# Attention scores divided at half the queries, products in other bursts, and loads in another order, in a fused attention and maxout feed-forward kernel

## The chip, the cores and the metric

One core of a Trainium2 chip runs the whole program. The metric is the device time of one execution in microseconds; the kernel before takes 307.9 us (median of three runs, 307.81 to 308.14). The engines are named as in the profile: PE multiplies matrices (PEld is its loading of weights), ACT evaluates functions such as Exp and Ln, DVE and POOL work on tiles elementwise, and SP issues transfers. ACT and POOL also issue transfers; those of POOL can convert float32 to bfloat16 on the way.

## The reference, cut to what matters

```python
# q, k, v: [8, 8, 576, 64]; beacon_k, beacon_v: [8, 8, 16, 64]
k_all = concatenate([beacon_k, k], axis=2)           # 592 keys
scores = scale * q @ k_all^T                         # beacons are seen by all, the rest causally
a = exp(scores - max); a /= a.sum(-1) + 1e-9
x = (a @ v_all) -> [8*576, 8*64]                     # 4608 tokens of 512
h = maximum(maximum(x @ w1, x @ w2), x @ w3)         # [4608, 768]
out = h @ w_out                                      # [4608, 512]
```

## The kernel before

**Quads.** The heads of a batch are taken four at a time. There are 16 such quads Q (two to a batch); PE works on four heads at once, each on 32 of its rows (scores) or 32 of its columns (products). Keys lie on the partitions in five tiles t of 128 (the last has 80 rows), queries along the free axis. `turn` lets DVE transpose the loaded q and k of a quad into `qT` and `kT`, in four pieces per quad.

**Four bursts to a quad.** `emit_scores(Q, c)` computes one burst c of the scores on PE (first 496 columns for each head, then 368, 464 and 336), ACT takes the exponential into `at_sb` in two instructions of two heads each, and POOL sets what a query may not see to zero (`affine_select`). `bursts` says which key tile and which range of queries belong to each burst.

**Products.** `pv_pass(Q, hf, part)` takes one half `hf` of the queries (288). Part 0 multiplies by ones and gives the row sums: ACT takes Ln and then Exp of its negative, which leaves the reciprocal in `recip`. Parts 1 and 2 multiply by v (even and odd columns) and DVE multiplies the result by `recip` into `xT` (L292). The first half of the queries costs 512 columns of PE in a pass, the second 1152. `PV_ORDER` makes three steps of two passes each, done in bursts 1, 2 and 3 of the next quad: both sums, then the two products of the first half, then the two of the second. Results lie in the tile `pv`, of which `pv_psum` holds two; a third pass reuses the buffer of the pass two before it.

**Feed-forward units.** When a batch is through attention, its tokens go through the feed-forward part in units of four to six products: `mm1_unit` (L311; i = 0 is copied by ACT, L319; i = 1 and 2 are joined by DVE, L321) and `mm2_unit` (L328; DVE copies the result to `y`, L336, and SP sends it out). There are 198 units of them. Unit results have two buffers, `fps`. `emit_all` writes the order of the work out by hand: in each burst it lets as many units follow as a counter allows (two per burst in quads 2 to 4, then 2.8), interleaved with the entries of `plan` (transposes, casts and loads, set by `at_step(Q, c, ...)`). Every engine runs its instructions in the order in which they are written.

**Opening.** `begin` loads q and k of quads 0 and 1 by SP in float32 and casts them on ACT, DVE and POOL; later quads come through POOL's queue with conversion (`load_qk16`, two to three quads ahead). V comes by SP in float32 (`load_v`) and is cast by POOL. Feed-forward units begin with quad 2.

Of the kernel before, what the change touches and what calls it, by code (L numbers as in the profile page):

```python
# [16 lines left out]
def kernel(  # L17
# [13 lines left out]
    nc = tc.nc  # L31
# [85 lines left out]
    def load_beacon_k(b0, b1, queues):  # L117
        for g, queue in enumerate(queues):
# [5 lines left out]
    def cast_beacon_k(b0, b1, cast):  # L124
        cast(bk16[:, b0:b1], bk32[:, b0:b1])

    def turn_beacon_k(b0, b1):
        nc.vector.transpose(
            bkT[:, b0:b1].rearrange("p b n e -> p (b n e)").bitcast(U32),
            bk16[:, b0:b1].rearrange("p b d -> p (b d)").bitcast(U32),  # L130
        )
# [66 lines left out]

    def load_w(i):
        wv = (moe_w1, moe_w2, moe_w3)[i].rearrange("(g p e) f -> p g (e f)", g=n_quad, e=2)  # L200
        nc.gpsimd.dma_start(out=w_in[i].rearrange("p (g e) f -> p g (e f)", e=2), in_=wv)
# [8 lines left out]
    def emit_scores(Q, c):  # L210
# [5 lines left out]
        off = 0  # L216
        for t, q0, q1 in bursts[c]:
            w = q1 - q0
            for j in range(2):
                for h in range(HG):  # L220
                    hs = slice(32 * h, 32 * h + 32)
                    nc.tensor.matmul(  # L222
                        sc[h // 2][:, h % 2, off : off + w],
                        kT[hs, 128 * t : 128 * (t + 1), j],
                        qT[hs, q0:q1, j],
                        start=(j == 0),
                        stop=(j == 1),
                        tile_position=(32 * h, 0),
                    )
            off += w  # L230
        a0, a1 = burst_at[c]
        for i in range(HG // 2):
            nc.scalar.activation(  # L233
                out=at_sb[:, 2 * i : 2 * i + 2, a0:a1],
                in_=sc[i][:, :, 0:off],
                func=AF.Exp,
                scale=scale,
            )
        off = a0
        for t, q0, q1 in bursts[c]:  # L240
            edge = min(q1, 128 * t - Nb + k_rows[t])
            if q0 == q_min[t]:
# [15 lines left out]
    def pv_pass(Q, hf, part):  # L258
# [25 lines left out]
        if part == 0:  # L284
# [4 lines left out]
            recips[hf] = recip  # L289
        else:  # L290
            c0 = b % RING * S + h0
            nc.vector.tensor_mul(xT[:, 2 * g + part - 1, c0 : c0 + HALF], ps, recips[hf])  # L292

    PV_ORDER = [(0, 0), (1, 0), (0, 1), (0, 2), (1, 1), (1, 2)]

    def emit_pv(Q, step):
        for hf, part in PV_ORDER[2 * step : 2 * step + 2]:
            pv_pass(Q, hf, part)
# [75 lines left out]
    def begin():  # L374
        load_beacon_k(0, 1, (nc.scalar, nc.gpsimd))
        load_qk(0, 1, (0, SH, QS))
        load_qk(0, 0, (0, SH, QS))
        load_qk(1, 1, (0, QS))
        load_qk(1, 0, (0, QS))
        load_v(0)  # L380
        cast_beacon_k(0, 1, by_pool)
        for which in (1, 0):
            for s0, s1 in ((0, SH), (SH, QS)):
                cast_qk(0, which, by_act, s0, s1)
                turn(0, which, s0, s1)
            if which == 1:
                turn_beacon_k(0, 1)
                put_beacon_k(0, by_dve)
                put_beacon_k(1, by_dve)
        cast_qk(1, 1, by_dve)  # L390
        turn(1, 1, 0, SH)
        turn(1, 1, SH, QS)
        cast_qk(1, 0, by_pool)
        load_beacon_k(1, B, (nc.sync, nc.sync))

    at_step(0, 0, L(turn, 1, 0, 0, SH), L(turn, 1, 0, SH, QS))
    at_step(0, 2, L(load_qk16, 2, 1), L(load_qk16, 2, 0), L(cast_v, 0, 0, 2, by_dve))
    at_step(0, 3, L(load_w, 0), L(cast_v, 0, 2, 4, by_dve))
    at_step(1, 0, L(cast_v, 0, 4, 5, by_pool), L(load_w, 1))
    at_step(1, 1, L(load_w, 2), L(cast_beacon_k, 1, B, by_pool), L(turn_beacon_k, 1, B))  # L400
    at_step(1, 2, L(load_qk16, 3, 1), L(load_qk16, 3, 0), L(load_v, 1))
    at_step(1, 3, L(load_w_out))
    for Q in range(2, NQ):
        b, g = divmod(Q, n_quad)
        at_step(Q - 1, 1 if Q > 2 else 3, L(turn, Q, 1, 0, SH))
        at_step(Q - 1, 2, L(put_beacon_k, Q, by_pool))
        at_step(Q - 1, 2 if Q > 2 else 3, L(turn, Q, 1, SH, QS), L(turn, Q, 0, 0, SH))
        at_step(Q - 1, 3, L(turn, Q, 0, SH, QS))
        if Q >= 4:
            at_step(Q - 3, 3, L(load_qk16, Q, 1), L(load_qk16, Q, 0))  # L410
        if g == 1:
            if b >= 2:
                at_step(Q - 4, 3, L(load_v, b))
# [4 lines left out]
    def emit_all():  # L418
# [8 lines left out]
        for Q in range(NQ):  # L427
            b, g = divmod(Q, n_quad)
            for c in range(NC):
                if Q == n_quad and c == 0:  # L430
                    for step in range(3):
                        emit_pv(Q - 1, step)
                    ready = 0
                elif Q > 0 and c > 0 and Q != n_quad:
                    emit_pv(Q - 1, c - 1)
                emit_scores(Q, c)
# [3 lines left out]
                allowed += early_rate if step in early else rate if step >= early.stop else 0.0  # L440
                for fn in plan.pop((Q, c), ()):
# [6 lines left out]
        assert not plan, list(plan)  # L448
        for step in range(3):
            emit_ffn(len(units), B - 2)  # L450
            emit_pv(NQ - 1, step)
# [38 lines left out]
```

## Time and profile before

| | before |
|---|---|
| median of three runs | 307.9 us |
| the profiled execution: time, span | 308.23 us, 306.5 us |
| PE busy | 278.5 us, 91% of the span |
| DVE, ACT, POOL busy | 54%, 52%, 29% |
| first feed-forward product | 36.82 us |
| chain that ended last: PE, ACT, transfers | 76%, 11%, 5% |
| PE's idle time before scores, unit products, attention products (v, ones) | 14.2, 6.6 and 1.7, 1.6 us |

The span is what the trace covers; 1.7 us of the execution's own time lie around it. In a row of a timeline stand the start, the time, the engine, the line, the operation, what it writes and reads, and in brackets the idle time of the engine just before, with what ended it. A row can merge several instructions; their count follows the x.

### The profile page before, as it was taken

The page shows a single profiled execution, that of the slowest core. Times are in us where ns is not written, and L with a number is a line of the kernel's source. Part 1 is how long each engine was busy: PE and PEld are TensorE (multiplying, and loading weights), DVE is VectorE, ACT ScalarE, POOL GpSimd, SP SyncE. Part 2 cuts the span into 40 slices and gives each one's busy share as a digit, 9 for nine tenths or more (in the row PEclk, how much of TensorE's full clock was granted, in tenths as well). Part 3 has the DMA queues.
Part 4 walks back from the last instruction along what each step waited for, and adds up shares of the span by engine and source line. Part 5 has one row for each costly group of instructions (what it writes and reads, how often), then busy time and mean ns, then how long its engine had stood idle before and what let it go on. Part 6 is the DMA issues. An engine that isn't in the chain of part 4 may idle for free.

```text
span 306.5 us, 7641 instructions
## 1 busy us (share of the span) xinstructions
PE 278.5 (91%) x3240; PEld 136.9 (45%) x3240; DVE 164.9 (54%) x282; ACT 159.2 (52%) x251; POOL 88.2 (29%) x159
## 2 busy tenths in 40 slices
PE   0477799998999999998999889999999999999995
PEld 0233534443454444443445657444444445444442
DVE  2603436855665566664647364755456456455553
ACT  4475597655765485645564637357545741220210
POOL 3356345434232432242323413242204210000000
PEclk9999999999999999999999999999999999999999
DMA  7979999995941495239333664250021002102103
GB/s 253 214 127 216 209 200 200 184 264 113 177 72 52 117 179 95 58 112 183 53 75 139 114 123 79 105 107 8 3 86 53 2 2 79 60 0 103 36 0 138
DMA packets 51650, 33.65 MB, mean 110 GB/s; under 512 B 41120, under 2 KB 41888, under 8 KB 51616
## 3 DMA queue, kind: packets, MB, share of 16 engines
q1 hardware_dynamic: 45728, 21.73, 28.7%
q0 software_dynamic: 5760, 11.42, 21.6%
q8 instruction: 25, 0.41, 0.6%
q14 instruction: 9, 0.07, 0.1%
q10 hardware_dynamic: 128, 0.02, 0.0%
HBM read 35.13 MB, written 9.44 MB: 145 GB/s over the span
## 4 chain that ended last, share of the span: by engine, by line
PE 76%; ACT 11%; DMA 5%; SPq 4%; DVE 1%; issue 1%; POOL 1%; DVEq 0%
PE fps L311 35%; PE fps L328 13%; PE pv L276 13%; PE sc L222 9%; ACT at_sb L233 7%; PE sc L311 5%; SPq L184 2%; DMA vst<-in_v_dram 2%; ACT hT L319 2%; PE sc L328 2%; DMA st<-in_q_dram 2%; DMA out_dram<-y 1%; SPq L122 1%; ACT lnd L286 1%; DVE xT L292 1%
## 5 line engine op out<-in xcount | busy, mean ns | idle before, releaser
L311 PE MATMUL fps<-xT,w_sb 128*128 128x512 bf16 (+1 forms) x648 | 140.1, 356 | 6.6 <-ACT hT L319 4.6
L233 ACT ACTIVATE at_sb<-sc 128x992 bf16<-128x992 f32 (+3 forms) x128 | 103.6, 863 | 76.9 <-PE sc L222 76.9
L321 DVE TENSOR_TENSOR hT<-hT,fps 128x512 bf16<-128x512 bf16 x96 | 65.9, 687 | 78.3 <-PE fps L311 46.7
L311 PEld LDWEIGHTS <-w_sb 128*128 128x128 bf16 x720 | 66.3, 98 | 81.0 <-issue 23.6
L245 POOL TENSOR_SCALAR_AFFINE_SELECT at_sb<-at_sb 128x512 bf16<-128x512 bf16 (+2 forms) x80 | 46.5, 590 | 150.5 <-ACT at_sb L233 150.4
L222 PE MATMUL sc<-qT,kT 32*128 32x288 bf16 (+4 forms) x768 | 41.1, 300 | 14.2 <-DVE qT L166 9.4
L319 ACT CAST hT<-fps 128x512 bf16<-128x512 f32 x48 | 28.1, 598 | 34.5 <-PE fps L311 34.4
L328 PE MATMUL fps<-w_out_sb,hT 128*128 128x512 bf16 x192 | 44.6, 380 | 0.0
L336 DVE COPY y<-fps 128x512 f32<-128x512 f32 x32 | 22.1, 692 | 21.5 <-PE fps L328 19.9
L276 PE MATMUL pv<-at_sb,v_sb 128*32 128x288 bf16 (+4 forms) x1024 | 31.4, 267 | 1.7 <-DVE xT L292 1.6
L328 PEld LDWEIGHTS <-hT 128*128 128x128 bf16 x216 | 20.3, 98 | 26.0 <-issue 2.7
L276 PEld LDWEIGHTS <-v_sb 128*32 128x32 bf16 (+1 forms) x1024 | 23.1, 101 | 16.7 <-issue 13.8
L222 PEld LDWEIGHTS <-kT 32*128 32x128 bf16 x768 | 16.2, 96 | 31.8 <-issue 17.0
L292 DVE TENSOR_TENSOR xT<-pv,recip 128x288 bf16<-128x288 f32 x64 | 26.9, 449 | 6.4 <-PE pv L276 3.9
L166 DVE STREAM_TRANSPOSE kT<-c 128x256 uint32<-128x256 uint32 (+1 forms) x32 | 22.2, 709 | 7.0 <-ACT c L159 3.5
L166 DVE STREAM_TRANSPOSE qT<-c 128x256 uint32<-128x256 uint32 (+1 forms) x32 | 21.8, 701 | 1.7 <-POOL c L159 1.4
L192 POOL CAST v_sb<-vst 128x1024 bf16<-128x1024 f32 (+1 forms) x22 | 19.4, 881 | 3.1 <-DMA vst<-in_v_dram 3.1
L311 PE MATMUL sc<-xT,w_sb 128*128 128x512 bf16 x72 | 18.5, 380 | 0.0
L286 ACT ACTIVATE lnd<-pv 128x288 f32<-128x288 f32 x32 | 12.9, 405 | 8.8 <-PE pv L276 8.7
L276 PE MATMUL pv<-at_sb,ones 128*32 128x288 bf16 (+4 forms) x512 | 16.0, 268 | 1.6 <-POOL at_sb L245 1.6
L276 PEld LDWEIGHTS <-ones 128*32 128x32 bf16 (+1 forms) x512 | 11.0, 100 | 9.7 <-issue 8.2
L288 ACT ACTIVATE recip<-lnd 128x288 f32<-128x288 f32 x32 | 14.2, 443 | 1.0
(24 smaller groups left out, 53.1 us busy)
## 6 DMA issues: line engine op xcount, KB each, us to landing
out_dram<-y SPq DMA_DIRECT2D x36, 256.0 KB, 2.0
vst<-in_v_dram SPq DMA_DIRECT2D x24, 256.0 KB, 5.4
c<-in_k_dram POOLq DMA_DIRECT2D x14, 288.0 KB, 4.4
c<-in_q_dram POOLq DMA_DIRECT2D x14, 288.0 KB, 5.3
w_sb<-in_moe_w_dram POOLq DMA_DIRECT2D x3, 768.0 KB, 10.6
vst<-in_v_dram SPq DMA_DIRECT2D x8, 224.0 KB, 4.5
vst<-in_v_dram SPq DMA_DIRECT2D x8, 160.0 KB, 6.1
w_out_sb<-in_moe_w_out_dram POOLq DMA_DIRECT2D x1, 768.0 KB, 14.6
```

What stands on the lines that cost most here:

```text
L166: nc.vector.transpose(dst.rearrange("p (t s) -> p s t", s=RUN)[:, s0:s1], src.rearrange("p (s d) -> p s d", d=DP),)
L192: cast(v_tiles[b][0:n, t0:t1].rearrange("p t h d -> p (t h d)"), stage["v", b][0:n, t0:t1].rearrange("p t h d -> p (t h d)"),)
L222: nc.tensor.matmul(sc[h // 2][:, h % 2, off : off + w], kT[hs, 128 * t : 128 * (t + 1), j], qT[hs, q0:q1, j], start=(j == 0), stop=(j == 1 ...
L233: nc.scalar.activation(out=at_sb[:, 2 * i : 2 * i + 2, a0:a1], in_=sc[i][:, :, 0:off], func=AF.Exp, scale=scale,)
L245: nc.gpsimd.affine_select(out=view, in_=view, compare_op=ALU.is_ge, fill=0.0, base=q0 - (128 * t - Nb), pattern=[[0, HG], [1, edge - q0]], ...
L276: nc.tensor.matmul(ps[32 * j : 32 * j + 32, lo - h0 : hi - h0], lhsT, at_sb[0:n, j, a : a + hi - lo], start=(i == 0), stop=(i == len(runs) ...
L292: nc.vector.tensor_mul(xT[:, 2 * g + part - 1, c0 : c0 + HALF], ps, recips[hf])
L311: nc.tensor.matmul(ps[:, o0 : o0 + n], w_in[i][:, ct, 128 * ft : 128 * (ft + 1)], xT[:, ct, x0 : x0 + n], start=(ct == 0), stop=(ct == n_c ...
L319: nc.scalar.copy(hT[:, ft, :], ps)
L321: nc.vector.tensor_max(hT[:, ft, :], hT[:, ft, :], ps)
L328: nc.tensor.matmul(ps, hT[:, ft, 128 * tt : 128 * (tt + 1)], w_out_sb[:, ft, :], start=(ft == 0), stop=(ft == n_ft - 1),)
L336: nc.vector.tensor_copy(y, ps)
```

## The change

**Bursts divided at half the queries.** A quad's four bursts are now: the first half of the queries for key tiles 0, 1 and 2 (512 columns per head), then the second half for tiles 0 and 3 (496), for tiles 1 and 4 (368) and for tile 2 (288). The total is the same, in eight pieces and not six, and six masks and not five. In quads 0 and 1 PE does two heads of a burst after the other two; from quad 2 on all four together as before.

**Products in other bursts.** From quad 3 on, burst 1 holds both products of the first half of the quad before, and then its sums of the second half; burst 3 holds both products of its second half, and then the sums of the first half of the present quad. Sums are so computed ahead of the products that need them. Bursts 0 and 2 hold none.

**A unit between exponents.** The first unit of a burst is written between the two exponentials of the burst and no longer behind them.

**Loads.** Beacon keys of batch 0 get tiles of their own, loaded on ACT's and SP's queues and turned by DVE. V of batch 1 comes through POOL's queue in bfloat16 (`load_v16`) with no cast. The loads of quads 2, 3 and 4 and of the weights are put in another order in that queue.

The order of PE in burst 1 of quad 5, before (one row for each kind of product and wait; pv with ones is a sum, pv with v_sb a product):

```order
L311 MATMUL fps_1257<-xT_68,w1_sb_62 128x512
L276 MATMUL pv_1263<-at_sb_960,ones_102 32x288
L276 MATMUL pv_1280<-at_sb_960,ones_102 32x288
L222 MATMUL sc_1305<-qT1_106,kT1_108 128x288 [waits Activation_49]
L222 MATMUL sc_1306<-qT1_106,kT1_108 128x80
L311 MATMUL fps_1327<-xT_68,w2_sb_63 128x512 [waits Activation_49]
```

and in the change:

```order
L367 MATMUL fps_1384<-xT_68,w1_sb_62 128x512
L315 MATMUL pv_1390<-at_sb_1061,v_sb_1244 32x288
L315 MATMUL pv_1404<-at_sb_1061,v_sb_1244 32x288
L315 MATMUL pv_1418<-at_sb_1061,ones_102 32x288 [waits DVE_49]
L256 MATMUL sc_1443<-qT1_106,kT1_108 128x288 [waits Activation_49]
L256 MATMUL sc_1444<-qT1_106,kT1_108 128x208
L367 MATMUL fps_1462<-xT_68,w2_sb_63 128x512 [waits Activation_49]
```

Three passes now stand together where two stood, and the third waits for DVE.

DVE between burst 2 and burst 3 of quad 5, before (hT is a unit's maximum, the transposes are for quad 6, and the xT rows multiply the products of the second half of quad 4):

```order
L321 TENSOR_TENSOR hT_1203<-hT_1203,fps_1387 128x512 [waits DVE_49,PE_49]
L166 STREAM_TRANSPOSE kT0_107<-c16_1_943 128x10x32
L166 STREAM_TRANSPOSE qT0_105<-c16_0_951 128x8x32 [waits DMASW1_49]
L321 TENSOR_TENSOR hT_1203<-hT_1203,fps_1401 128x512 [waits PE_49,Activation_49]
L292 TENSOR_TENSOR xT_68<-pv_1407,recip_1303 128x288 [waits PE_49]
L292 TENSOR_TENSOR xT_68<-pv_1429,recip_1303 128x288 [waits PE_49]
```

and in the change:

```order
L377 TENSOR_TENSOR hT_1318<-hT_1318,fps_1502 128x512 [waits DVE_49,PE_49]
L183 STREAM_TRANSPOSE kT0_107<-c16_1_1050 128x10x32
L377 TENSOR_TENSOR hT_1318<-hT_1318,fps_1518 128x512 [waits PE_49,Activation_49]
L183 STREAM_TRANSPOSE qT0_105<-c16_0_1052 128x8x32 [waits DMASW3_49]
L331 TENSOR_TENSOR xT_68<-pv_1525,recip_1441 128x288 [waits PE_49]
L331 TENSOR_TENSOR xT_68<-pv_1547,recip_1441 128x288 [waits PE_49]
```

The transpose of q stands behind the burst's last maximum now, directly ahead of the multiplications.

ACT in burst 3 of quad 4, before (lnd and recip are the reciprocal of the sums; the exponentials read sc; the copy to hT is of a unit):

```order
L233 ACTIVATE at_sb_960<-sc_1189 128x2x336 [waits PE_49]
L233 ACTIVATE at_sb_960<-sc_1190 128x2x336 [waits PE_49]
L319 CAST hT_1203<-fps_1204 128x512 [waits PE_49]
L233 ACTIVATE at_sb_1221<-sc_1222 128x2x496 [waits PE_49,Pool_49]
L233 ACTIVATE at_sb_1221<-sc_1223 128x2x496 [waits PE_49]
```

and in the change:

```order
L325 ACTIVATE lnd_1303<-pv_1290 128x288 [waits PE_49]
L327 ACTIVATE recip_1305<-lnd_1303 128x288 [waits DVE_49,Activation_49]
L267 ACTIVATE at_sb_1061<-sc_1307 128x2x288 [waits PE_49]
L375 CAST hT_1318<-fps_1319 128x512 [waits PE_49]
L267 ACTIVATE at_sb_1061<-sc_1308 128x2x288
```

The copy of a burst's first unit stands between the exponentials, and one pair of Ln and Exp stands ahead of them; in burst 1 there is one pair now where there were two.

The diff, cut to its core:

```diff
     bursts = [
-        [(0, 0, HALF), (3, q_min[3], S)],
-        [(0, HALF, S), (4, q_min[4], S)],
-        [(1, q_min[1], S)],
-        [(2, q_min[2], S)],
+        [(t, q_min[t], HALF) for t in range(3)],
+        [(0, HALF, S), (3, q_min[3], S)],
+        [(1, HALF, S), (4, q_min[4], S)],
+        [(2, HALF, S)],
     ]
...
+    def load_v16(b, t0, t1):
...
+            nc.gpsimd.dma_start(
+                out=v_tiles[b][lo : lo + n, t],
+                in_=v[b, :, k0 : k0 + n, :].rearrange("h p d -> p h d"),
+            )
...
+        for heads in ((0, 1), (2, 3)) if Q < n_quad else (range(HG),):
...
-    PV_ORDER = [(0, 0), (1, 0), (0, 1), (0, 2), (1, 1), (1, 2)]
...
+    pv_step(1, 1, (0, 0, 0), (0, 1, 0))
+    pv_step(1, 2, (0, 0, 1), (0, 0, 2), (1, 0, 0))
+    pv_step(1, 3, (0, 1, 1), (0, 1, 2))
+    for Q in range(2, NQ):
+        if Q > 2:
+            pv_step(Q, 1, (Q - 1, 0, 1), (Q - 1, 0, 2), (Q - 1, 1, 0))
+            pv_step(Q, 3, (Q - 1, 1, 1), (Q - 1, 1, 2))
+        pv_step(Q, 3, (Q, 0, 0))
+    pv_end = [
+        [(NQ - 1, 0, 1), (NQ - 1, 0, 2), (NQ - 1, 1, 0)],
+        [(NQ - 1, 1, 1), (NQ - 1, 1, 2)],
+    ]
...
     def begin():
-        load_beacon_k(0, 1, (nc.scalar, nc.gpsimd))
+        load_first_beacon_k(0, nc.scalar)
         load_qk(0, 1, (0, SH, QS))
         load_qk(0, 0, (0, SH, QS))
+        load_first_beacon_k(1, nc.sync)
         load_qk(1, 1, (0, QS))
         load_qk(1, 0, (0, QS))
         load_v(0)
...
         cast_qk(1, 0, by_pool)
+        load_qk16(2, 1)
+        load_qk16(2, 0)
+        load_w(0)
...
+            at_step(*(Q - 3, 3) if Q > 4 else (2, 2), L(load_qk16, Q, 1), L(load_qk16, Q, 0))
...
+                emit_pv(pv_at.pop((Q, c), ()))
+                if (Q, c) == (n_quad, 0):
+                    emit_pv([(Q - 1, 0, 1), (Q - 1, 0, 2), (Q - 1, 1, 0)])
+                emit_exp = emit_scores(Q, c)
...
+                emit_exp(0)
+                emit_ffn(allowed, ready)
+                emit_exp(1)
+                emit_masks(Q, c)
+                if (Q, c) == (n_quad, 0):
+                    emit_pv([(Q - 1, 1, 1), (Q - 1, 1, 2)])
+                    ready = 0
```

More of the change, by code (lines that the diff above doesn't have):

```diff
@@ L238, in emit_scores, with emit_masks @@
             )
[L239 removed]
+        return emit_exp
+    def emit_masks(Q, c):
+        at_sb = at[Q]
+        off = burst_at[c][0]
         for t, q0, q1 in bursts[c]:
             edge = min(q1, 128 * t - Nb + k_rows[t])
[L242 removed]
+            if edge > q0:
                 n = k_rows[t]
```

129 lines of the change are left out of this document (75 added, 54 removed).

## The prediction

> **What bounds the kernel now.** I read the busy shares first, then the chain of waits and PE's waits, then stretches of ten microseconds, and at last the timeline of one burst after another.
>
> ```profile
> PE 278.5 (91%) x3240; PEld 136.9 (45%) x3240; DVE 164.9 (54%) x282; ACT 159.2 (52%) x251; POOL 88.2 (29%) x159
> PE 76%; ACT 11%; DMA 5%; SPq 4%; DVE 1%; issue 1%; POOL 1%; DVEq 0%
> 20.00:30.00 10.00, 7.82 (x130) 4.21 (x128) 2.05 (x6) 6.46 (x10) 6.41 (x12) 1.00 1.11 216
> 80.00:90.00 10.00, 10.00 (x127) 4.56 (x126) 6.84 (x12) 5.35 (x8) 2.66 (x6) 1.00 0.69 117
> ```
>
> PE bounds it: no other engine is busy more than 54%, and from 80 to 90 us PE has no idle time that a row shows. Only the opening, until feed-forward units begin at 36.82, has PE free. So every microsecond that PE loses after the opening is added to the end, and what PE waits for now is the most that can be taken away there:
>
> ```profile
> PE fps L311 <- ACT hT L319: 4.6, 7, 0.8
> PE sc L222 <- ACT at_sb L233: 4.6, 8, 1.1
> PE fps L311 <- DVE xT L292: 1.2, 1, 1.2
> ```
>
> About 7 us in all, and part of the second row lies in the opening.
>
> **The third pass (the largest term).** The change puts three passes into bursts 1 and 3, while the tile pv has two buffers. PE's order shows that the third pass waits for DVE; the buffer it needs is that of the first pass of its own group, so it waits until DVE has multiplied that one into xT. Before, passes came in pairs, and the buffers were emptied a burst earlier, which is why PE waits for xT in pv only once:
>
> ```profile
> 26.90 0.78 DVE L292 TENSOR_TENSOR xT<-pv,recip 128x288 bf16<-128x288 f32 x2
> 27.37 2.11 PE L276 MATMUL pv<-at_sb,v_sb 128*32 128x288 bf16 x40 [1.62 <-DVE xT L292]
> L292 DVE TENSOR_TENSOR xT<-pv,recip 128x288 bf16<-128x288 f32 x64 | 26.9, 449 | 6.4 <-PE pv L276 3.9 <-ACT lnd L286 1.8 <-issue 0.4
> ```
>
> There PE starts at 27.37, some 0.05 after a multiplication of 0.42 to 0.45 us that began at 26.90. How late the multiplication is in the steady part is read from a step with both pairs:
>
> ```profile
> 160.57 0.63 PE L276 MATMUL pv<-at_sb,v_sb 128*32 128x288 bf16 x24
> 160.68 0.69 DVE L336 COPY y<-fps 128x512 f32<-128x512 f32 x1 [0.60 <-PE fps L328]
> 161.13 0.59 PE L222 MATMUL sc<-qT,kT 32*128 32x464 bf16 x8
> 161.29 0.81 DVE L292 TENSOR_TENSOR xT<-pv,recip 128x288 bf16<-128x288 f32 x2
> 163.77 0.77 DVE L166 STREAM_TRANSPOSE kT<-c 128x320 uint32<-128x320 uint32 x1
> 164.35 1.18 PE L276 MATMUL pv<-at_sb,v_sb 128*32 128x288 bf16 x40
> 164.45 0.69 DVE L336 COPY y<-fps 128x512 f32<-128x512 f32 x1
> 165.06 0.65 DVE L166 STREAM_TRANSPOSE qT<-c 128x256 uint32<-128x256 uint32 x1
> 165.46 0.48 PE L222 MATMUL sc<-qT,kT 32*128 32x336 bf16 x8
> 165.55 0.80 DVE L292 TENSOR_TENSOR xT<-pv,recip 128x288 bf16<-128x288 f32 x2
> ```
>
> Short pair (first half of the queries, now burst 1): the passes start at 160.57 and PE could issue a third about 0.46 later, a little before the 161.13 at which scores start now. The first multiplication stands behind the y copy of the last unit; it starts at 161.29 and ends 0.45 later, at 161.74. PE resumes at 161.79 instead of 161.03: a loss of 0.76. There are 13 such groups (quads 3 to 15) and one at the end: 14 x 0.75 = **10.5 us**, a little off since in some bursts ACT takes the last unit's result. The floor, with DVE free when the first pass ends: 0.13 (the remainder of a stretch, worked out below) + 0.21 (512 columns) + 0.45 + 0.05 - 0.46 = 0.38, 14 x 0.38 = 5.3.
>
> Long pair (second half, burst 3): the third pass could start 1.0 us after 164.35. The multiplication ends at 165.55 + 0.45 = 166.00, PE resumes at 166.05: a loss of 0.70. Here DVE was held by the last copy and the transpose of q. In a second such place the copy was later:
>
> ```profile
> 147.75 1.18 PE L276 MATMUL pv<-at_sb,v_sb 128*32 128x288 bf16 x40
> 149.41 0.80 DVE L292 TENSOR_TENSOR xT<-pv,recip 128x288 bf16<-128x288 f32 x2
> ```
>
> 149.41 + 0.45 + 0.05 - 148.75 = 1.16. In the new order the transpose of q stands right ahead of these multiplications in quads 3 to 14, as in these two rows. I take the mean, 0.93, for 12 quads and 0.24 for the last, which has no transposes (between the floor and 0.70 less part of 0.65): 12 x 0.93 + 0.24 = **11.4 us**. Floor with DVE free: 0.13 + 0.48 + 0.45 + 0.05 - 1.0 = 0.11, 13 x 0.11 = 1.4. Upper bound: where both transposes follow the last maximum (0.77 more than in the first place), 0.70 + 0.77 = 1.47, 13 x 1.47 = 19. What is late next is the Ln of the third pass and the exponentials behind it; ACT is half idle there, so I add nothing.
>
> **Fewer switches, more pieces.**
>
> ```profile
> 76.28 0.83 PE pv L276 x32
> 80.32 0.56 PE pv L276 x24
> 46.28 0.55 PE sc L222 x16
> 80.88 0.52 PE sc L222 x8
> 165.45 0.12 PEld L222 LDWEIGHTS <-kT 32*128 32x128 bf16 x8
> ```
>
> The 32 matmuls are 1664 columns per head and the 24 are 1024, so a column takes 0.27 us / 640 = 0.42 ns and each stretch of passes has about 0.13 us that no column explains. A quad has two stretches now where it had three: 14 x 0.13 = **-1.8 us**. The burst of 496 columns in two pieces takes 0.55 for two times 496 columns (0.42 us) and that of 464 in one piece 0.52 (0.39 us): the same remainder, so a second piece is nearly free. Lower bound 0, upper bound 0.12 per added piece (eight weight loads in the open). Two pieces more in each of 14 quads; the new piece of 48 columns is shorter than any here, so I take 0.03: **+0.8 us** (0 to 3.4). The sixth mask of a quad is POOL's, busy 29%.
>
> **A unit between exponents.** It removes the wait of a unit for its copy behind two exponentials, and delays the second exponential by one copy. The row above gives at most 4.6; part returns as scores that wait for the second exponential in burst 1, behind Ln, Exp, exponential and copy. Bounds -4.6 and +1; I take **-2.5 us**.
>
> **The opening.**
>
> ```profile
> 9.43 1.02 PE L222 MATMUL sc<-qT,kT 32*128 32x288 bf16 x16 [9.43 <-DVE qT L166]
> 13.19 1.46 ACT L233 ACTIVATE at_sb<-sc 128x736 bf16<-128x736 f32 x2 [0.83 <-PE sc L222]
> 15.33 1.78 ACT L233 ACTIVATE at_sb<-sc 128x928 bf16<-128x928 f32 x2 [0.68 <-PE sc L222]
> 30.20 1.35 ACT L233 ACTIVATE at_sb<-sc 128x672 bf16<-128x672 f32 x2 [3.00 <-PE sc L222]
> 36.82 1.90 PE L311 MATMUL fps<-xT,w_sb 128*128 128x512 bf16 x8
> ```
>
> The exponentials of quads 0 and 1 set the pace. Between bursts ACT waits 0.7 to 0.8 us for scores (two such rows of five), since the scores of all four heads wait for both buffers; with two heads at a time that goes. The wait of 3.00 goes too: it stems from the xT multiplication behind the beacon transpose, which the rows at 26.90 and 27.37 show. Scores begin some 0.7 earlier with a beacon load that DVE need not wait for. Together 7 to 8 us. Against it: k and q of quad 1 are requested behind four beacon loads on SP, each of which waits for an earlier transfer, some 3 us later than now, and the products of quad 1 and the scores with two heads at a time load PE more, at half speed: the 32 matmuls of sums at 20.02 take 1.58 us where those at 48.59 take 0.90.
>
> ```profile
> 20.02 1.58 PE L276 MATMUL pv<-at_sb,ones 128*32 128x288 bf16 x32
> 48.59 0.90 PE L276 MATMUL pv<-at_sb,ones 128*32 128x288 bf16 x32
> ```
>
> I take **-5 us** (first unit at about 31.8); bounds -8 and +1. [...]
>
> **Two waits that go, one that may come.**
>
> ```profile
> 69.77 0.69 DVE L336 COPY y<-fps 128x512 f32<-128x512 f32 x1 [1.50 <-PE sc L222]
> 71.36 1.60 PE L311 MATMUL fps<-xT,w_sb 128*128 128x512 bf16 x6 [1.16 <-DVE xT L292]
> 27.85 0.56 POOL L153 DMA_DIRECT2D c<-in_k_dram  x1
> 40.27 1.26 DVE L166 STREAM_TRANSPOSE kT<-c 128x256 uint32<-128x256 uint32 x2 [3.41 <-DMA c<-in_k_dram]
> ```
>
> At 69.77 the copy to y waited for an output transfer behind V loads, and PE 1.16 us behind it; V of batch 1 has left SP's queue, so **-1.2**. The 1.2 us at the end (row of xT above) go as well, since three units now stand behind the last products: **-1.2**. Against that, k of quad 3 took 12.4 us from its issue at 27.85 to its use. k of quad 4 was requested at 33 us and is now requested in quad 2, burst 2, near 38, behind V of batch 1 and two weights; its transpose comes near 47 and holds up every unit's maximum behind it. 0 to 6 us, I take **+2**.
>
> **The sum.** 10.5 + 11.4 - 1.8 + 0.8 - 2.5 - 5 - 1.2 - 1.2 + 2 = +13.0 us. On the profiled execution's 308.2 that is 321.2; the median stands 0.3 below it, so **321 us**.
>
> **Rivals.**
> *Late loads.* k and q of quads 4 and 5 and V of batch 2 share transfers that are full from 20 to 70 us (a share above 1 in the row 20 to 30). If quad 4's pieces land at 55 and not at 49, units stop for 8 us: 329. For it speaks the 12.4 us above; against it, that POOL's queue starts 3 us earlier.
> *DVE keeps up (faster).* If DVE reaches the multiplication as soon as a group's first pass ends, third passes cost their floor, 5.3 + 1.4 = 6.7, and not 21.9; the rest of the sum is -8.9, for 308.2 + 6.7 - 8.9 = 306. It decides where the mean of the 27 waits falls under 8.9 / 27 = 0.33. For it: DVE is busy 54% and PE's new gaps give it time. Against it: the last maximum or copy of a burst always ends after the pass has begun (160.68 and 164.45 and 0.69 each).
> *The waits cost nothing.* If another buffer were free, the sum without 21.9 is 299. PE's order speaks against it.
> [...]
>
> **Chances.** Forecast 0.70, late loads 0.10, DVE keeps up 0.12, no cost 0.02, half speed 0.03, a sum that comes out at no change 0.03. The forecast's own range is 312 to 329 by the bounds of the two largest terms and the opening. To leave out no more than 2 in 10 I reach to 305 and 331. A measurement of this kernel cannot tell 0.2% (0.6 us) from no change. Faster 0.14, same 0.03, slower 0.83.
>
> **What would show it.** In the new profile PE's wait for xT before pv should stand at about 22 us in some 27 times, in burst 1 about 0.75 each and in burst 3 near 0.9. PE's wait for hT should fall below 4.6; the y wait near 70 should be gone; the first unit should start near 31.8, and ACT's gaps of 0.7 to 0.8 before 20 us be gone. The forecast is wrong if PE's waits for xT sum to under 9 us, or if the first unit starts after 36.

## The result and the profile after

The change makes the kernel slower: 323.6 us (median, 322.7 to 323.8) where the kernel before took 307.9 beside it, a ratio of 1.051, 95% interval 1.048 to 1.053. The forecast was 321, in a range of 305 to 331. The profiled execution took 323.68 us, with a span of 321.9. Where one of a kernel's executions ran in a slower state of the chip (393.85 us with a third buffer, 316.16 with long groups alone), medians and ratios here leave it out.

The busy shares and the chain of waits of the changed kernel, from its page:

```profile
PE 278.5 (87%) x3462; PEld 146.9 (46%) x3496; DVE 166.2 (52%) x290; ACT 160.7 (50%) x251; POOL 90.1 (28%) x172
PE 71%; DVE 11%; DMA 8%; issue 3%; ACT 3%; SPq 2%; POOL 0%; DVEq 0%
```

Two of its stretches of ten microseconds (the length, then busy time of PE, PEld, DVE, ACT and POOL, and at the end the granted clock, the share of the transfer engines and GB/s):

```profile
25.00:35.00 10.00, 9.05 (x184) 5.79 (x184) 5.09 (x14) 6.09 (x10) 0.95 (x3) 0.50 1.50 184
80.00:90.00 10.00, 9.19 (x141) 4.76 (x141) 5.84 (x10) 5.25 (x9) 3.05 (x7) 1.00 0.95 180
```

And PE's waits (in all, times, longest):

```profile
PE pv L315 <- DVE xT L331: 23.7, 28, 4.0
PE sc L256 <- DVE qT L183: 9.9, 3, 8.4
PE sc L256 <- ACT at_sb L267: 1.5, 4, 0.6
```

PE's busy time is the same to the tenth, 278.5 us. From 80 to 90 us it was busy throughout before and is now idle for 0.81 us. DVE's share of the chain has gone from 1% to 11%. In the waits, the rows for ACT's hT copies (4.6) and for xT behind an output copy (1.2) are gone, and a row of 23.7 us is new: PE ahead of a pass, for xT. Of its 28 times two lie in the opening (4.03 and 0.52); the other 26 sum to 19.1 us, 0.74 each: 14 in short groups, 0.35 to 0.66 and 0.57 on average, and 12 in long groups, 0.53 to 1.32 and 0.93 on average. The long group of the last quad shows none.

One of each kind of group, from the timeline of quad 4 (start, time, engine, line, what it writes and reads, and in brackets the idle time just before):

```profile
48.29 0.63 PE L315 MATMUL pv<-at_sb,v_sb 128*32 128x288 bf16 x24
48.47 0.69 DVE L377 TENSOR_TENSOR hT<-hT,fps 128x512 bf16<-128x512 bf16 x1 [0.18 <-PE fps L367]
49.07 0.82 DVE L331 TENSOR_TENSOR xT<-pv,recip 128x288 bf16<-128x288 f32 x2
49.58 0.68 PE L315 MATMUL pv<-at_sb,ones 128*32 128x288 bf16 x20 [0.66 <-DVE xT L331]
50.19 0.62 PE L256 MATMUL sc<-qT,kT 32*128 32x288 bf16 x16
...
55.28 1.17 PE L315 MATMUL pv<-at_sb,v_sb 128*32 128x288 bf16 x40
56.20 0.75 DVE L183 STREAM_TRANSPOSE kT<-c 128x320 uint32<-128x320 uint32 x1
56.80 0.63 DVE L183 STREAM_TRANSPOSE qT<-c 128x256 uint32<-128x256 uint32 x1
57.28 0.81 DVE L331 TENSOR_TENSOR xT<-pv,recip 128x288 bf16<-128x288 f32 x2
57.77 0.40 PE L315 MATMUL pv<-at_sb,ones 128*32 128x288 bf16 x12 [1.32 <-DVE xT L331]
```

In the short group (above) the multiplication stands behind a unit's maximum, begins at 49.07 and ends its first half near 49.5; PE's third pass, the sums, begins at 49.58. In the long group both transposes of the next quad stand ahead of it. In both, PE restarts a few hundredths after the first of two multiplications ends (49.07 + 0.45 and 57.28 + 0.44, for 49.58 and 57.77).

### The profile page after: what moved, and what is told of

Read it like the earlier page. It is cut to its first block, busy times and chain, and to the rows that moved or that the text cites. A ratio compares the mean times of both kernels' runs of the same rounds, so it can differ in the third digit from the quotient of the medians.

```text
span 321.9 us, 8131 instructions
## 1 busy us (share of the span) xinstructions
PE 278.5 (87%) x3462; PEld 146.9 (46%) x3496; DVE 166.2 (52%) x290; ACT 160.7 (50%) x251; POOL 90.1 (28%) x172
## 4 chain that ended last, share of the span: by engine, by line
PE 71%; DVE 11%; DMA 8%; issue 3%; ACT 3%; SPq 2%; POOL 0%; DVEq 0%
PE fps L367 35%; PE fps L384 13%; PE pv L315 8%; PE sc L256 8%; PE sc L367 5%; DVE hT L377 4%; DMA vst<-in_v_dram 4%; DMA c<-in_k_dram 3%; DVE xT L331 3%; DVE qT L183 2%; ACT at_sb L267 2%; PE sc L384 2%; SPq L201 2%; DMA st<-in_q_dram 1%; DVE y L392 1%
## 5 line engine op out<-in xcount | busy, mean ns | idle before, releaser
L367 PE MATMUL fps<-xT,w_sb 128*128 128x512 bf16 (+1 forms) x621 | 133.5, 355 | 3.2 <-issue 2.7
L267 ACT ACTIVATE at_sb<-sc 128x1024 bf16<-128x1024 f32 (+3 forms) x128 | 105.5, 859 | 30.7 <-PE sc L256 30.1
L367 PEld LDWEIGHTS <-w_sb 128*128 128x128 bf16 x720 | 66.3, 98 | 68.6 <-issue 9.8
L284 POOL TENSOR_SCALAR_AFFINE_SELECT at_sb<-at_sb 128x448 bf16<-128x448 bf16 (+2 forms) x96 | 49.2, 528 | 164.5 <-ACT at_sb L267 155.3
L256 PE MATMUL sc<-qT,kT 32*128 32x288 bf16 (+4 forms) x1024 | 43.2, 268 | 11.9 <-DVE qT L183 9.9
L375 ACT CAST hT<-fps 128x512 bf16<-128x512 f32 x48 | 28.0, 584 | 34.1 <-PE fps L367 34.1
L384 PE MATMUL fps<-w_out_sb,hT 128*128 128x512 bf16 x187 | 43.9, 379 | 0.4 <-issue 0.2
L256 PEld LDWEIGHTS <-kT 32*128 32x128 bf16 x1024 | 24.5, 97 | 33.1 <-issue 16.9
L315 PE MATMUL pv<-at_sb,ones 128*32 128x288 bf16 (+4 forms) x512 | 18.7, 269 | 23.8 <-DVE xT L331 23.7
L315 PEld LDWEIGHTS <-v_sb 128*32 128x32 bf16 (+1 forms) x1024 | 22.4, 101 | 15.3 <-issue 11.9
L315 PEld LDWEIGHTS <-ones 128*32 128x32 bf16 (+1 forms) x512 | 13.9, 99 | 29.1 <-issue 15.8
L367 PE MATMUL sc<-xT,w_sb 128*128 128x512 bf16 x71 | 18.4, 379 | 0.1
L209 POOL CAST v_sb<-vst 128x1024 bf16<-128x1024 f32 (+1 forms) x18 | 16.0, 892 | 0.0
## 6 DMA issues: line engine op xcount, KB each, us to landing
w_sb<-in_moe_w_dram POOLq DMA_DIRECT2D x3, 768.0 KB, 10.2
```

Of the source, the lines that this page charges most:

```text
L209: cast(v_tiles[b][0:n, t0:t1].rearrange("p t h d -> p (t h d)"), stage["v", b][0:n, t0:t1].rearrange("p t h d -> p (t h d)"),)
L256: nc.tensor.matmul(sc[h // 2][:, h % 2, off : off + w], kT[hs, 128 * t : 128 * (t + 1), j], qT[hs, q0:q1, j], start=(j == 0), stop=(j == 1 ...
L267: nc.scalar.activation(out=at_sb[:, 2 * i : 2 * i + 2, a0:a1], in_=sc[i][:, :, 0 : a1 - a0], func=AF.Exp, scale=scale,)
L284: nc.gpsimd.affine_select(out=view, in_=view, compare_op=ALU.is_ge, fill=0.0, base=q0 - (128 * t - Nb), pattern=[[0, HG], [1, edge - q0]], ...
L315: nc.tensor.matmul(ps[32 * j : 32 * j + 32, lo - h0 : hi - h0], lhsT, at_sb[0:n, j, a : a + hi - lo], start=(i == 0), stop=(i == len(runs) ...
L367: nc.tensor.matmul(ps[:, o0 : o0 + n], w_in[i][:, ct, 128 * ft : 128 * (ft + 1)], xT[:, ct, x0 : x0 + n], start=(ct == 0), stop=(ct == n_c ...
```

## The experiments

Ratios are to the kernel before, timed beside each run; brackets hold 95% intervals. Diffs are cut to their core.

### Undo the groups of three: pairs again

```diff
-            pv_step(Q, 1, (Q - 1, 0, 1), (Q - 1, 0, 2), (Q - 1, 1, 0))
-            pv_step(Q, 3, (Q - 1, 1, 1), (Q - 1, 1, 2))
-        pv_step(Q, 3, (Q, 0, 0))
+            pv_step(Q, 1, (Q - 1, 0, 0), (Q - 1, 1, 0))
+            pv_step(Q, 2, (Q - 1, 0, 1), (Q - 1, 0, 2))
+            pv_step(Q, 3, (Q - 1, 1, 1), (Q - 1, 1, 2))
...
```

The products of the last quad, at the end, are put in three pairs too.

> The changed kernel with its passes of quads 3 to 15 in pairs again (both sums in burst 1, the first half's products in burst 2, the second half's in burst 3; three pairs at the end); divided bursts, the unit between exponents and all loads stay. Theory (the third pass waits for DVE): the waits of about 22 us go, 1.8 us of switches and some of PE's waits for ACT's copies come back, 303 to 307 us. Rival (the time is lost to the divided bursts, the sixth mask or ACT's new order, and the third pass only takes over time that PE would have waited anyway): 318 us or more.

Measured: 303.9 us, 0.987 [0.981, 0.992]. From 323.6 that is 20 us, and the kernel is now 1.3% faster than the one before. The trace is of the fastest of four executions (300.6 us; the others took 303.8 to 304.2). PE's waits:

```profile
PE pv L315 <- DVE xT L331: 3.9, 3, 1.8
PE fps L368 <- ACT hT L376: 0.5, 2, 0.2
```

What is left of the xT row lies before 53 us. The rest of the change (divided bursts, loads, the unit between exponents) is a gain.

### Keep groups of three, but the sums first

```diff
-            pv_step(Q, 1, (Q - 1, 0, 1), (Q - 1, 0, 2), (Q - 1, 1, 0))
-            pv_step(Q, 3, (Q - 1, 1, 1), (Q - 1, 1, 2))
-        pv_step(Q, 3, (Q, 0, 0))
+            pv_step(Q, 1, (Q - 1, 1, 0), (Q - 1, 0, 1), (Q - 1, 0, 2))
+        pv_step(Q, 3, (Q, 0, 0))
+        if Q > 2:
+            pv_step(Q, 3, (Q - 1, 1, 1), (Q - 1, 1, 2))
...
```

> The changed kernel with the sums as the first and not the third pass of each group, in quads 3 to 15 and at the end: the third pass then waits for ACT's Ln (0.41 us) of a pass that ended long ago and not for DVE's multiplication of xT. Theory: about 0.35 us left in a group with two short passes and 0.05 in one with two long ones, 5.5 us in place of 22, so 304 to 310 us. Rival (three passes in a row cost their time whatever empties the buffer, or the time is lost elsewhere): 318 us or more.

Measured: 312.0 us, 1.016 [1.010, 1.021]: 11.6 us faster than the change, but above the 304 to 310 expected. The third pass now waits for the Ln of the sums on ACT, which is done sooner than a multiplication behind DVE's queue (waits of 0.3 us at most, for 0.35 to 1.32 in the change):

```profile
PE pv L315 <- ACT lnd L325: 3.9, 14, 0.3
PE pv L315 <- DVE xT L331: 5.9, 2, 5.4
```

and in the timeline, behind the opening:

```profile
62.47 0.64 PE L256 MATMUL sc<-qT,kT 32*128 32x288 bf16 x24 [1.87 <-DVE qT L183]
63.04 2.89 PE L368 MATMUL fps<-xT,w_sb 128*128 128x512 bf16 x8
```

So the steady part did what was expected: 14 waits of 0.28 in place of 26 of 0.74. The miss lies ahead of it, in the opening (a wait of 5.4 us) and at 62 us, where a wait of 1.87 is followed by eight products in 2.89 us that elsewhere take 1.90.

### Put one group of three into the kernel before

```diff
-        for hf, part in PV_ORDER[2 * step : 2 * step + 2]:
+        for hf, part in PV_ORDER[(0, 2, 5)[step] : (2, 5, 6)[step]]:
```

> The kernel before with one pass moved: burst 2 takes both products of the first half and the first product of the second, burst 3 the last alone. Nothing else differs. Theory: 14 groups whose third pass waits 0.76 us for xT, 10.6 us, less what PE's waits for ACT's copies (4.6 us) shrink: 313 to 319 us. Rival (DVE keeps up, or the wait only replaces another): 307 to 309 us.

Measured: 319.6 us, 1.040 [1.038, 1.042], a loss of 12.2 us, just above the 313 to 319 expected. Here the third pass is a product, not a sum:

```profile
PE pv L276 <- DVE xT L292: 12.0, 15, 3.7
PE fps L311 <- ACT hT L319: 4.6, 7, 0.8
```

One is the opening's 3.7; fourteen share 8.3 us of idle time. From the start of the last matmul before to the start of the next they cost 0.61 to 0.84 each, near 11 us. So a third pass costs this in the order before too, whatever its kind. The wait for ACT did not shrink.

### The change without the unit between the exponents

```diff
                 emit_exp(0)
-                emit_ffn(allowed, ready)
                 emit_exp(1)
```

> The changed kernel with both exponentials of a burst together again and the first unit behind them. By the prediction's term the unit between them is worth 2.5 us: 326 us. Rival, from the new trace, where PE no longer waits for ACT's copies at all: the pauses of the third passes give ACT time to catch up, the place of the unit is worth under 1 us here: 323 to 324.6 us.

Measured: 327.3 us, 1.066 [1.061, 1.072]. The row "PE fps L367 <- ACT hT L375: 6.7, 14, 0.9" is back and 3.7 us are lost by the medians, so the unit between the exponents is worth more than the 2.5 of the prediction. A wait of 3.9 us at 52.6, for a late hT, muddies the figure; in quads 6 to 14, behind it, the loss is 5.2 us (the table further down).

### The unit between the exponents alone, in the kernel before

The exponentials and masks become functions that are called apart, as in the change:

```diff
+                emit_exp(0)
+                emit_ffn(allowed, ready)
+                emit_exp(1)
+                emit_masks(Q, c)
```

> The kernel before with one part of the change alone: the FFN unit between the two exponents of a group, nothing else. Theory: this is the part that gains, and by more than the 2.5 us of the prediction: PE's waits for ACT's hT copies (4.6 us by idle time, 9.2 us from start to start) vanish. Expected 301 to 305. Rival: exponents that come later make the next scores wait by as much, 306.5 to 308.5.

Measured: 304.0 us, 0.988 [0.983, 0.992], a gain of 3.8 us by the ratio. Of the 4.6 us of PE's wait for ACT's hT copies 0.2 is left. This one edit of a few lines holds nearly all that the pairs above gained over the kernel before. In quads 6 to 14 it gains 6.9 us, and quad 6 begins 2.6 us later than before: part of the steady gain is lost ahead of it.

### A third buffer for the passes

```diff
-    pv_psum = ctx.enter_context(tc.tile_pool(name="pv_psum", bufs=2, space=PSUM))
-    ffn_psum = ctx.enter_context(tc.tile_pool(name="ffn_psum", bufs=2, space=PSUM))
+    pv_psum = ctx.enter_context(tc.tile_pool(name="pv_psum", bufs=3, space=PSUM))
+    ffn_psum = ctx.enter_context(tc.tile_pool(name="ffn_psum", bufs=1, space=PSUM))
```

> The changed kernel with its order untouched and three PSUM buffers for the passes instead of two; the third is taken from the FFN units, which have one instead of two. Theory: the third pass of a group waits only because both buffers are still read by DVE, so PE's waits for xT before a pass fall from 23.7 us to below 6 (the opening's 4 remain). The single FFN buffer costs where units follow one another closely (up to 7 us over 200 units). Expected 303 to 313. Rival: the order itself costs (more switches and shorter runs), the xT waits are only where the time is booked, and the run stays at 318 or more.

Measured: 388.4 us, 1.264 [1.256, 1.272]. Half of the expectation came true, the time not at all:

```profile
PE fps L367 <- DVE hT L377: 41.4, 62, 0.8
PE fps L367 <- ACT hT L375: 22.3, 34, 0.8
PE fps L384 <- DVE y L392: 13.0, 20, 0.8
PE pv L315 <- DVE xT L331: 2.3, 1, 2.3
```

With three buffers and the order untouched the third passes don't wait any more (23.7 to 2.3, and that one lies in the opening). A short group in the steady part shows it directly:

```profile
106.35 0.63 PE L315 MATMUL pv<-at_sb,v_sb 128*32 128x288 bf16 x24
106.81 0.66 PE L315 MATMUL pv<-at_sb,ones 128*32 128x288 bf16 x20
106.82 0.82 DVE L331 TENSOR_TENSOR xT<-pv,recip 128x288 bf16<-128x288 f32 x2 [1.48 <-PE pv L315]
```

The third pass starts 0.46 us after the first, before DVE has multiplied anything. So the wait is for the buffer and for nothing else in the order. But the units follow one another in twos and threes, and with one buffer each waits for the copy of the one before: 76.7 us in three rows of 0.65 to 0.67 a time. I had put that at up to 7. Where the buffer was taken from counted for more here than where it went.

### The opening of the change: V's last cast on POOL

```diff
-    at_step(0, 3, L(cast_v, 0, 4, 5, by_dve), L(load_qk16, 3, 1), L(load_qk16, 3, 0))
-    at_step(1, 0, L(load_v16, 1, 0, 1))
+    at_step(0, 3, L(load_qk16, 3, 1), L(load_qk16, 3, 0))
+    at_step(1, 0, L(cast_v, 0, 4, 5, by_pool), L(load_v16, 1, 0, 1))
```

In the change DVE stands at this cast, and PE behind it:

```profile
24.10 0.42 DVE L209 CAST v_sb<-vst 80x512 bf16<-80x512 f32 x1 [6.44 <-DMA vst<-in_v_dram]
24.94 0.80 DVE L331 TENSOR_TENSOR xT<-pv,recip 128x288 bf16<-128x288 f32 x2
25.43 0.62 PE L315 MATMUL pv<-at_sb,ones 128*32 128x288 bf16 x12 [4.03 <-DVE xT L331]
35.26 1.67 PE L367 MATMUL fps<-xT,w_sb 128*128 128x512 bf16 x7 [0.16 <-issue]
```

> The changed kernel with one move in the opening: the cast of the last V tile of the first batch is done by POOL one group later (as in the kernel before) and no longer by DVE. In the changed kernel DVE stands 6.44 us for this tile's transfer, and everything queued behind it (kT, xT) is late, so that PE waits 4.03 us for xT before a third pass and its granted clock then falls to 0.5 for 10 us. Theory: this one stall is what the prediction's opening term missed. Expected: no wait above 1.5 us before a third pass, first FFN unit at 31 to 32 us instead of 35.3, no fall of the clock, and 319 to 321 us. Rival: the transfer is late for the products too, the wait only moves to another reader of V, first unit at 34 to 36, 323 to 324 us.

Measured: 322.7 us, 1.050 [1.044, 1.056], not to be told from the change. The stall at 25 us did go, and the first unit starts at 28.69 for 35.26. But what was won came back 25 us later:

```profile
28.69 1.90 PE L367 MATMUL fps<-xT,w_sb 128*128 128x512 bf16 x8
51.12 0.66 DVE L183 STREAM_TRANSPOSE kT<-c 128x256 uint32<-128x256 uint32 x1 [3.31 <-DMA c<-in_k_dram]
53.88 0.80 DVE L331 TENSOR_TENSOR xT<-pv,recip 128x288 bf16<-128x288 f32 x2
54.38 0.62 PE L315 MATMUL pv<-at_sb,ones 128*32 128x288 bf16 x12 [3.88 <-DVE xT L331]
55.53 3.59 PE L367 MATMUL fps<-xT,w_sb 128*128 128x512 bf16 x8
```

The k of quad 4 comes when the transfers bring it: DVE waits 3.31 us for it where it waited 0.76 in the change, PE behind it 3.88 for 1.32, and then PE runs eight products in 3.59 us for 1.90. Neither theory had this: the wait moved, but to another tensor.

### Pairs with a mended opening

The pairs above, the last V cast on POOL, and:

```diff
-    at_step(2, 0, L(load_v16, 1, 3, 5), L(load_w, 2))
-    at_step(2, 1, L(load_w_out))
+    at_step(2, 0, L(load_qk16, 4, 1), L(load_qk16, 4, 0), L(load_v16, 1, 3, 5))
+    at_step(2, 1, L(load_w, 2))
+    at_step(2, 2, L(load_w_out))
...
                 emit_exp(0)
+                if Q > 0 and c == 3:
+                    for fn in plan.pop((Q, c), ()):
+                        fn()
                 emit_ffn(allowed, ready)
```

> The changed kernel with passes in pairs again from quad 3 on, the last V cast of the first batch on POOL, the k and q of quad 4 loaded ahead of V and the last weights, and the last turn of q of a quad put on DVE ahead of the group's first hT product. Theory: with pairs, what is left above the sum of PE's work are single waits for DVE in quads 3 and 4 (0.76, 1.17 and 1.34 us: qT at 42, xT at 52 behind a late k, qT at 57), so 299 to 302, below the pairs alone (303.9). Rival: the waits are set by the transfers of the opening as a whole and only move, 303 to 305.

Measured: 301.2 us, 0.978 [0.975, 0.982]. The waits at 42, 52 and 57 us are gone; the one that is left lies at 27.6 (2.88, for xT behind the beacon keys of batch 1). How much it gains over the pairs alone stays open, since one execution of those took 300.6. It serves as the ground for the next four runs.

### Each group of three by itself

Long groups only (the sums of the first half third, behind the products of the second half; the other sums alone in a burst):

```diff
-            pv_step(Q, 1, (Q - 1, 0, 0), (Q - 1, 1, 0))
-            pv_step(Q, 2, (Q - 1, 0, 1), (Q - 1, 0, 2))
+            pv_step(Q, 1, (Q - 1, 0, 1), (Q - 1, 0, 2))
+            pv_step(Q, 2, (Q - 1, 1, 0))
             pv_step(Q, 3, (Q - 1, 1, 1), (Q - 1, 1, 2))
+        pv_step(Q, 3, (Q, 0, 0))
...
```

> The pairs with the mended opening (301.15 us), with one group of each quad made as in the changed kernel: the two products of the second half and, third, the sums of the next quad's first half (long groups, beside the fourth burst); the sums of the second half stand alone in the group before, so that the short group stays two products. Theory: each third pass waits until DVE has freed the buffer of the first product, in this group behind a turn of q or an hT product too, so 12 to 13 waits of some 1.1 us: 313 to 316. By the term of the prediction (0.93 each, 11.4 in all) 312.5. Rival: the changed kernel's third passes cost time only where they come twice in a quad, since PE gives the first wait back within the quad; then 304 to 309.

Short groups only:

```diff
-            pv_step(Q, 1, (Q - 1, 0, 0), (Q - 1, 1, 0))
-            pv_step(Q, 2, (Q - 1, 0, 1), (Q - 1, 0, 2))
+            pv_step(Q, 0, (Q - 1, 0, 0))
+            pv_step(Q, 1, (Q - 1, 0, 1), (Q - 1, 0, 2), (Q - 1, 1, 0))
...
```

> The pairs with the mended opening (301.15 us), with the other group of each quad made as in the changed kernel: the two products of the first half and, third, the sums of the second half (short groups, beside the second burst); the sums of the first half stand alone in the quad's first group, so that the long group stays two products. Theory: DVE is mostly free here, so 14 waits of 0.5 idle, 0.78 from start to start: 310.5 to 313.5. By the term of the prediction (0.75 each, 10.5 in all) 311.7. Rival: as for the long groups, 303 to 308.

Measured: long 312.5 us, 1.018 [1.011, 1.025]; short 311.9 us, 1.013 [1.008, 1.019]. Against the 0.978 of the pairs that is 0.040 and 0.035 of 307.5 us: **12.2 and 10.7 us**, each good to about 2. The prediction had 11.4 and 10.5. The long run also has a wait, at 50 us, that the pairs and the short run lack:

```profile
PE fps L369 <- DMA w_sb<-in_moe_w_dram: 4.6, 1, 4.6
```

So whole times mix the price of a group with another opening. From the first exponential of quad 6 to that of quad 15, nine quads with nine groups of each kind, every run does the same work (53 hT maxima, 27 hT copies, 20 copies to y):

| run | quad 6 begins at, us | quads 6 to 14, us |
|---|---|---|
| before | 89.1 | 147.3 |
| before, a unit between the exponents | 91.7 | 140.4 |
| before, one group of three | 92.0 | 154.4 |
| the change | 94.7 | 155.9 |
| the change, exponents together | 95.7 | 161.1 |
| the change, sums first | 95.3 | 145.2 |
| pairs | 87.6 | 141.0 |
| pairs with the mended opening | 87.2 | 141.6 |
| long groups alone | 90.4 | 150.1 |
| short groups alone | 91.3 | 148.6 |

Runs with the same order in these quads agree to 0.1 us (V's cast on POOL 155.9 like the change; the two runs of the next section 141.6). Here a long group costs 8.4 us, **0.94 each**, and a short one 7.0, **0.77 each**, where the prediction had 0.93 and 0.75. The two together, 15.4, are a little more than the 14.3 to 14.9 between the change and either run with pairs, so each price stands by itself: PE does not give one wait back in the other group.

### Weights later, and V of later batches later

First, on the pairs with the mended opening, the first two expert weights start later (from the beginning and the second group to the third and the fifth):

```diff
-        load_w(0)
...
-    at_step(0, 1, L(load_w, 1))
-    at_step(0, 2, L(cast_v, 0, 0, 2, by_dve), L(cast_v, 0, 2, 4, by_dve))
+    at_step(0, 2, L(load_w, 0), L(cast_v, 0, 0, 2, by_dve), L(cast_v, 0, 2, 4, by_dve))
...
-    at_step(1, 0, L(cast_v, 0, 4, 5, by_pool), L(load_v16, 1, 0, 1))
+    at_step(1, 0, L(cast_v, 0, 4, 5, by_pool), L(load_w, 1), L(load_v16, 1, 0, 1))
```

> The pairs with the mended opening (301.15 us), and the first two expert weights started later in POOL's queue: the first two groups later, the second behind the last V cast of batch 0. Theory: from 12 us on the opening's transfers run at a steady 205 to 225 GB/s and share it, so that V's last tile and the second batch's beacon keys land late (24.1, 28.6); with 1.5 MB of weights behind them they land some 3 us earlier, PE's wait of 2.9 us at 27.6 goes and with it the half clock after it: 297.5 to 300.5. Rival: the wait moves to the weights (the first FFN unit waits), 301 to 304.

Then, on top of it:

```diff
-            at_step(Q - 4, 3, L(load_v, b))
+            at_step(Q - 2, 0, L(load_v, b))
```

> The pairs with the mended opening and the first weights later, and the V of batches 2 and 3 (1.2 MB each) loaded seven groups later (at the first group of the third quad of the batch before, not at the last group of the quad before that). Theory: the opening is held by the sum of its transfers: from 10 to 60 us they run at a steady 180 to 240 GB/s, and a gain at the first FFN unit (29.3 us for 34.2) was given back at 46 us as a wait of 4.4 us for the third weight, issued at 35.1 and landed at 50. The two V loads stand in that stretch (27 to 62 us) and are first read near 65 us; without them the weight lands before its unit, the wait and the half clock after it go: 301.96 less 4.4 and some 1 to 2: 295 to 298. Rival: the weight's transfer is slow by itself (13 us from issue to landing for 768 KB in many small packets), the wait stays: 300 to 302.

Measured: 302.0 us, 0.982 [0.979, 0.986], and 300.8 us, 0.979 [0.977, 0.982]. The first moves the first unit from 34.2 to 29.3 us and gains nothing; now PE waits for the third weight. Its row in PE's waits:

```profile
PE fps L368 <- DMA w_sb<-in_moe_w_dram: 4.4, 1, 4.4
```

and stretches of the same run, with the transfer rate in the last column:

```profile
20.00:30.00 10.00, 8.12 (x220) 5.37 (x214) 6.10 (x15) 7.88 (x13) 7.00 (x12) 1.00 1.09 202
40.00:50.00 10.00, 5.87 (x102) 3.04 (x102) 4.50 (x9) 6.63 (x10) 4.23 (x9) 0.95 1.31 185
50.00:60.00 10.00, 9.39 (x93) 4.29 (x96) 5.51 (x10) 2.36 (x4) 0.47 (x1) 0.71 1.16 204
```

The second did take that wait away, as expected, but its time is that of the pairs with the mended opening, not the 295 to 298 expected: a wait of 2.2 us for xT at 26 us and one of 1.2 at 49 stand in its place, and from 50 us on PE has no more than 0.4 us in ten left to give (rows 9.64, 9.66, 9.99 and 10.00 from 50 to 90). Which transfers set the opening's end, and how early it could be, stays open; three orders of them gave 301.2, 302.0 and 300.8.

## Why the prediction was right

**The third pass** was the largest term, +21.9 us, and it was right in its place, its cause and its size. The changed kernel's row says 23.7 us in 28 times, 19.1 without the opening (idle time alone). The runs with one kind of group say 10.7 for the short (10.5 predicted) and 12.2 for the long (11.4), and in the nine quads of the table 0.77 and 0.94 each (0.75 and 0.93). In a short group the row counts less than the price: 0.57 of idle time for 0.77. The buffer as its cause is shown by the run with three, where the row all but vanishes with the order untouched. The rivals "DVE keeps up" (a mean wait under 0.33; it was 0.74) and "the waits cost nothing" are out. What carried this term was a question put to the old timeline: where is DVE when the first pass of a group ends?

**The unit between exponents** was too small at -2.5: in the kernel before, that part alone gains 3.8, and without it the change loses 3.7. In quads 6 to 14 alone it is 6.9 and 5.2, beyond the 4.6 that I had called the most. PE's waits in those quads before sum to 4.9 in the rows; where the other 2 us went stays open. What I set against it, scores that wait for the second exponential, did not come in the steady part (that row is 1.5 us in the change, for 4.6; with this part alone it is 6.5, but only 0.2 of it lies behind 60 us).

**The opening** is the step that failed, though the total came out near. I took -5 and the first unit at 31.8; it came at 35.26, -1.6. The terms on ACT and the beacon keys held: the first scores start at 8.40 for 9.43, and ACT's gaps of 0.7 to 0.8 are down to 0.2 and 0.3. What I missed is that the order puts the cast of V's last tile on DVE, in front of the transposes and xT, while that tile lands at 24.10. I had read which loads change their queue, not which engine then waits for the last of them. And even without that stall the gain is mostly not kept, as three runs show (V's cast on POOL, weights later, V later; in the first of them 6.6 us at the first unit have shrunk to 1.6 where quad 6 begins): from 10 to 60 us the transfers run at 173 to 232 GB/s (stretches of ten microseconds of the change and of the last two runs), and a PE that was earlier waited at the next tensor: 3.88 us behind the k of quad 4, 4.4 for the third weight, 2.2 and 1.2 for xT. In the change quad 6 begins 5.6 us later than before; the six third passes ahead of it are worth about 5 of that by the prices above, so nothing of the 5 us is left there.

**A late k of quad 4** was put at +2. In the change it costs DVE 0.76 us (idle before the transpose at 54.51), part of the longest steady waits. It became 3.3 once the opening was mended. "Late loads", as a rival of 329, did not come about; but late tensors show in the openings: DVE waits 3.4 us for k in the kernel before and 6.4 for V in the change, PE 4.4 for a weight with the weights later.

**The two waits that go** were one. The row of 1.2 us for xT and the gap of 1.16 at 71.36 are the same event ("1.2, 1, 1.2" says one time), and I took it off twice; the forecast should have been 1.2 higher for that alone. Not foreseen either: 0.76 and 0.70 us of scores that wait for the transpose of q at the start of quads 3 and 4:

```profile
45.89 0.64 PE L256 MATMUL sc<-qT,kT 32*128 32x288 bf16 x24 [0.76 <-DVE qT L183]
61.07 0.64 PE L256 MATMUL sc<-qT,kT 32*128 32x288 bf16 x24 [0.70 <-DVE qT L183]
```

**More pieces** cost close to nothing: these 24 matmuls of 512 columns take 0.64 where 16 matmuls of 496 columns take 0.62 (the row at 50.19 above). In quads 6 to 14 the pairs take 0.6 us more than the unit alone in the kernel before, and that difference holds the pieces, the sixth mask and DVE's other order together; of the +0.8, about 0.5 falls on these quads.

**The sum**, with what was measured in place of what was taken: third passes +1.0, unit between exponents -1.3, opening +3.4, the wait counted twice +1.2, q +1.5, k at the end of quad 3 about -1.2 to -2: +3.8 to +4.6, where the time missed the forecast by 2.6. It closes to about 2 us, as well as the single prices are known.

**That the total is so near is in part luck.** For quads 6 to 14 the terms give 9 x 0.75 + 9 x 0.93 = 15.1 for the third passes, -1.2 for the switches, +0.5 for the pieces and -2.5 for the unit between exponents (PE's waits for ACT's copies all lie there before): +12.0. Measured is +8.6. For the rest of the time they give +1.0, and measured is +6.8 (5.6 ahead of quad 6, 1.1 behind quad 14). A miss of over 3 us one way and one of nearly 6 the other way, the unit and the opening above all, leave 2.6. One figure of the working does not come out of its own parts: the bounds of the two largest terms and the opening give 303 to 335 and not 312 to 329.

**Half speed** of PE behind the new gaps, at 0.03 in the chances, did not come in the steady part: 26 waits of 0.35 to 1.3 us, and the granted clock stays at 1.00 from 35 to 320 us. In the opening it did fall, to 0.50 between 25 and 35 us; the last section has that.

## What to carry to other kernels

Before putting three passes that share two buffers into one group, find in the old timeline where the engine that empties them stands at the end of the first pass. Here, with PE busy 91% of the span, the lag read there (0.75 and 0.93 us) was paid once for each group (0.77 and 0.94). Putting first the pass whose buffer ACT empties cut the waits of the steady part from 19.1 us to 3.9, and taking the buffer from the units brought 76.7 us of waits where third passes had brought 23.7. Of the 6.6 us won at the first unit with V's cast on POOL 1.6 were left where quad 6 begins: ask what the faster engine meets next, and whether that comes earlier too.

## What the runs showed of the hardware

PE's granted clock stayed full behind the short gaps of these runs and fell behind the longer ones named here. In the run with one FFN buffer PE waits 116 times for the copy of a unit, 0.66 us on average, in stretches like this one, and behind the opening the clock column stays at 1.00:

```profile
100.00:110.00 10.00, 7.40 (x105) 3.59 (x105) 3.75 (x7) 5.55 (x8) 3.03 (x6) 1.00 0.36 61
```

So did it after single gaps of 1.05 us (V's cast on POOL, at 43 us), 1.32 (the change), 1.34 (pairs) and 1.35 (weights later). After gaps of 4.03 (the change), 3.88 (V's cast on POOL), 2.88 (pairs, mended opening) and 1.87 (sums first, at 62 us) it fell to 0.5 for 10.2, 6.8, 3.4 and 3.4 us. How long it stayed down did not follow from the gap: 4.61 us (long groups alone) brought 3.4, and 1.99 (the unit alone) 10.2. The stretch after the gap of 3.88:

```profile
55.00:60.00 5.00, 5.00 (x40) 1.83 (x40) 2.06 (x3) 1.93 (x4) 1.50 (x3) 0.50 0.81 174
```

PE is busy in all of it, with products of 0.45 us each for 0.24: a stall of 3.9 us cost 1.7 more in the first eight products behind it. Early in the opening the column can't be read: in the kernel before it says 1.00 from 20 to 30 us, where 32 matmuls of sums take 1.58 us that later take 0.90.
